# A convolution band read from a padded tap row in DRAM, early x in fp32 by a hardware queue, a smaller first weight chunk, and w_out issued early

## The chip, the cores and the metric

The kernel runs on one core of a Trainium2 chip. The metric is the device time of one execution in microseconds (us). Medians are over runs interleaved with runs of the kernel before on the same chip. A time is longer than the span of the profiled execution by 1.7 to 2.0 us; in a few runs by 2.1 to 3.5, which no profile explains. I compare kernels by times and locate the difference by spans.

## The reference

```python
# x: (8, 4096, 192) f32; weight: (8 heads, 7 taps); w_in: (192, 2048); w_out: (2048, 192)
w = softmax(weight, axis=-1)                       # per head
y[b, s, d] = sum_k w[head(d), k] * x_pad[b, s + k, d]   # causal, 6 zeros in front, 24 channels a head
h = y.reshape(32768, 192) @ w_in
g = where(h > 0, h, exp(min(h, 0)) - 1)
out = g @ w_out
```

## The kernel before

The tokens are cut into 32 blocks of 1024. A block needs 16 "pairs": for each of 16 slices of 128 hidden columns, six matmuls (three steps for each of two row tiles of 64) make two PSUM banks of h. ScalarE takes exp, GpSimd clips, VectorE joins the branches into gT (fp16), and TensorE multiplies gT by w_out. Three PSUM slots of two banks rotate among pairs and convolutions.

From block 1 on, the convolution is a matmul of x by a banded matrix, 40 small matmuls for half a block. Its result goes out of PSUM (`csb`), through DRAM (`conv_slots`) and back in another layout (`att`): the bounce. Block 0 takes another way, which needs no band and is quicker to start: x is transposed and multiplied by diagonal matrices ("the head").

What the change and the argument touch (cuts marked by `...`):

```python
# SP: the band, three transfers through DRAM
sy.dma_start(wq[...], <weight broadcast to 128 partitions>).then_inc(s_wq, 16)
W(s_tz, 1); W(s_w[0], 32)
sy.dma_start(band[:, :, :], Tm[:, :, :]).then_inc(s_band, 16)      # zeros
W(s_band, 16); W(s_set, 5)
sy.dma_start(diagonal, wprb[:]).then_inc(s_band, 16)               # taps, scattered on a diagonal
W(s_band, 32)
sy.dma_start(Tm[:], band[:, :, :]).then_inc(s_band, 16)            # the band comes back
...
# GpSimd: the software DMA queue, in this order
load_head(0); load_head(1)                   # x, cast to bf16
load_w_in(0); load_w_in(1); <xg of block 1>; load_w_in(2)
for n in range(NP):
    if n == W_OUT_AT:  <load w_out>          # W_OUT_AT = 8
    ...
# TensorE, at each item of the order
if m == 0: W(s_band, 48)                     # first convolution waits for the band
pe.matmul(H[...], xg[:, s % NXB, w, CPH*h:CPH*(h+1)], Tm[:, h, PAD+c0 : PAD+c0+nc_], ...)
...
elif n < NQ - 1: warm(WARM[1])               # block 0 only: two warming matmuls between pairs
```

## Time and profile before

| what | value |
|---|---|
| time, median of 4 runs | 760.12 us (759.85 to 763.15) |
| span of the profiled run | 758.2 us |
| TensorE busy | 742.6 us, 98% |
| first transposes / first pair / pair 16 | 8.42 / 15.42 / 43.27 us |

The prediction shows how these lines are read. The point is the last row: all of the slack lies before pair 16, the first pair of block 1, after which TensorE is full.

### The profile page before, as it was taken

The numbers are of one execution on the slowest core, as the hardware profiler recorded it, in microseconds if no ns is written. First come the engines' busy times: TensorE is split into PE (matmuls) and PEld (weight loads), VectorE is DVE, ScalarE is ACT, GpSimd is POOL, SyncE is SP. The second block draws the span as 40 slices with busy tenths as digits, with TensorE's granted clock in tenths as the row PEclk, the third lists the DMA queues.
The fourth block names the chain that finished last, engine by engine and source line by source line (L and its number), as shares of the span: only waits on it lengthen the run. The fifth ranks groups of instructions, "written<-read, shape, count | busy, mean of one in ns | idle before, by whom it ended". The sixth has DMA issues, their size and how long they took to land.

```text
span 758.2 us, 32332 instructions
## 1 busy us (share of the span) xinstructions
PE 742.6 (98%) x13911; PEld 513.4 (68%) x13911; DVE 636.8 (84%) x1043; ACT 646.9 (85%) x1161; POOL 660.6 (87%) x1107
## 2 busy tenths in 40 slices
PE   6889999999999999999999999999999999999997
PEld 4256676676767667667667667667667667667676
DVE  3778988988988988988988988988988988988993
ACT  3778888888888888888888888888888889889882
POOL 4879989989988988988988998988988998988892
PEclk9999999999999999999999999999999999999999
DMA  9643453443453453453453454354354354354112
GB/s 144 108 84 94 102 114 77 104 103 85 101 116 77 100 111 80 100 116 81 96 108 87 95 116 87 90 116 82 92 116 95 82 116 86 89 115 104 61 44 64
DMA packets 107135, 72.77 MB, mean 96 GB/s; under 512 B 44784, under 2 KB 106736, under 8 KB 106992
## 3 DMA queue, kind: packets, MB, share of 16 engines
q1 hardware_dynamic: 66344, 54.03, 23.6%
q0 software_dynamic: 40304, 16.47, 19.7%
q8 instruction: 109, 1.79, 1.0%
q14 instruction: 34, 0.28, 0.1%
q10 hardware_dynamic: 344, 0.20, 0.1%
HBM read 45.43 MB, written 41.71 MB: 115 GB/s over the span
## 4 chain that ended last, share of the span: by engine, by line
PE 95%; DMA 2%; ACT 1%; DVE 1%; POOL 1%; issue 0%; SPq 0%; POOLq 0%
PE H L628 44%; PE ops L657 44%; PE H L604 5%; DMA conv_slots<-csb 1%; DMA xh<-in_x_dram 1%; PE H L657 1%; DVE gT L499 0%; DMA att<-conv_slots 0%; PE ops L531 0%; ACT E L427 0%; PE H L579 0%; POOL E L351 0%; PE ops L579 0%; PE H L560 0%; SPq L279 0%
## 5 line engine op out<-in xcount | busy, mean ns | idle before, releaser
L499 DVE SCALAR_TENSOR_TENSOR gT<-E,H 128x512 f16<-128x512 f32 x1024 | 631.0, 682 | 98.4 <-POOL E L351 90.9
L351 POOL TENSOR_SCALAR E<-E 128x512 f32<-128x512 f32 x1024 | 604.0, 612 | 82.9 <-ACT E L427 79.3
L427 ACT ACTIVATE E<-H 128x512 f32<-128x512 f32 x1024 | 546.2, 605 | 87.4 <-PE H L628 73.8
L657 PEld LDWEIGHTS ops<-w_out,gT 64*128 64x128 f16 x8064 | 342.4, 94 | 109.6 <-ACT osb L405 10.9
L657 PE MATMUL ops<-w_out,gT 64*128 64x192 f16 x8064 | 414.4, 243 | 0.9 <-DVE gT L499 0.9
L628 PE MATMUL H<-att,w_in 64*128 64x512 bf16 x3072 | 407.3, 378 | 5.1 <-DVE gT L499 3.2
L628 PEld LDWEIGHTS H<-att,w_in 64*128 64x128 bf16 x3072 | 129.6, 94 | 107.2 <-DVE gT L499 6.0
L416 ACT ACTIVATE csb<-H 128x1024 bf16<-128x1024 f32 x62 | 63.5, 1024 | 0.0
L405 ACT ACTIVATE osb<-ops 128x768 f32<-128x768 f32 x63 | 51.6, 819 | 5.1 <-PE ops L657 5.1
L307 POOL DMA_DIRECT2D xg<-in_x_dram x62 | 52.2, 842 | 0.4 <-issue 0.4
L604 PE MATMUL H<-Tm,xg 128*24 128x122 bf16 (+1 forms) x2480 | 40.7, 209 | 0.7 <-DVE gT L499 0.7
L604 PEld LDWEIGHTS H<-Tm,xg 128*24 128x24 bf16 x2480 | 31.3, 92 | 11.3 <-issue 10.7
L531 PE MATMUL ops<-zw 128*128 128x512 bf16 x35 | 11.6, 434 | 1.2 <-DVE zw L438 1.2
L510 DVE COPY osb<-H 128x384 f32<-128x384 f32 x1 | 0.6, 558 | 8.9 <-PE H L657 8.9
L531 PEld LDWEIGHTS ops<-zw 128*128 128x128 bf16 x35 | 2.5, 106 | 7.5 <-issue 6.0
L657 PE MATMUL H<-w_out,gT 64*128 64x192 f16 x128 | 5.6, 243 | 0.1
L657 PEld LDWEIGHTS H<-w_out,gT 64*128 64x128 f16 x128 | 5.2, 94 | 0.3 <-PE H L657 0.3
L548 PE MATMUL H<-ident,xh 128*64 128x2 bf16 x12 | 0.8, 192 | 4.0 <-DMA xh<-in_x_dram 4.0
L397 ACT ACTIVATE osb<-H 128x384 f32<-128x384 f32 x1 | 0.5, 490 | 4.7 <-PE H L657 4.7
L548 PEld LDWEIGHTS H<-ident,xh 128*64 128x64 bf16 x12 | 0.7, 151 | 4.9 <-issue 4.9
L312 POOL DMA_DIRECT2D w_in<-in_moe_w_in_dram x6 | 3.8, 642 | 0.0
L463 DVE CAST xT<-H 128x512 bf16<-128x512 f32 x1 | 0.7, 692 | 3.5 <-PE H L560 3.5
(41 smaller groups left out, 26.4 us busy)
## 6 DMA issues: line engine op xcount, KB each, us to landing
out_dram<-osb SPq DMA_DIRECT2D x127, 192.0 KB, 2.7
conv_slots<-csb SPq DMA_DIRECT2D x62, 256.0 KB, 2.5
att<-conv_slots SPq DMA_DIRECT2D x186, 64.0 KB
xg<-in_x_dram POOLq DMA_DIRECT2D x31, 240.0 KB, 5.1
xg<-in_x_dram POOLq DMA_DIRECT2D x31, 192.0 KB, 4.4
w_in<-in_moe_w_in_dram POOLq DMA_DIRECT2D x4, 288.0 KB, 10.1
w_out<-in_moe_w_out_dram POOLq DMA_DIRECT2D x1, 768.0 KB, 9.9
xh<-in_x_dram POOLq DMA_DIRECT2D x2, 192.0 KB, 5.5
```

What stands on the lines that cost most here:

```text
L307: g.dma_start(xg[:, b, w0:w1, :], src).then_inc(s_x[b][part - 1], 16)
L312: g.dma_start(w_in[HP * r : HP * (r + 1), :, c0:c1], moe_w_in.rearrange("(p j) f -> p j f", j=3)[:, :, c0:c1],).then_inc(s_w[k], 16)
L351: g.tensor_scalar(out=E[:, n % NE, u, :], in0=E[:, n % NE, u, :], scalar1=1.0, scalar2=0.0, op0=ALU.min, op1=ALU.max,).then_inc(s_clp)
L405: a.activation(osb[:, b, :, :, :].rearrange("p g k d -> p g (k d)"), ops[:, :, 0 : 2 * D], ACT.Copy,).then_inc(s_oev)
L416: a.activation(csb[:, m % 4, :, :], H[:, slot_of_conv[m] % 3, :].rearrange("p (b t) -> p b t", b=2), ACT.Copy,).then_inc(s_ce)
L427: a.activation(E[:, n % NE, u, :], H[:, k, GS * u : GS * (u + 1)], ACT.Exp).then_inc(s_exp)
L499: v.scalar_tensor_tensor(out=gT[:, s % NG3, q, u, :], in0=E[:, n % NE, u, :], scalar=1.0, in1=H[:, slot_of_pair[n] % 3, GS * u : GS * (u + ...
L531: pe.matmul(ops[:, 0, :], zw[:, 0:P], zw[:], start=True, stop=True)
L548: ins = pe.matmul(halos()[HP:P, j, i, 0:HALO], xh[:, 0, i, j::3], ident[:, P - HALO : P], start=True, stop=True, tile_position=(0, HP),)
L604: ins = pe.matmul(H[SLOT * q : SLOT * q + CPH, k % 3, GS * hb + o : GS * hb + o + nc_], xg[:, s % NXB, w, CPH * h : CPH * (h + 1)], Tm[:, ...
L628: ins = pe.matmul(H[:, k % 3, GS * r : GS * (r + 1)], w_in[HP * r : HP * (r + 1), j, FC * q : FC * (q + 1)], att[HP * r : HP * (r + 1), s ...
L657: ins = pe.matmul(acc[:, g, D * kb : D * (kb + 1)], gT[HP * rt : HP * (rt + 1), t % NG3, q, g, t0 : t0 + P], w_out[HP * rt : HP * (rt + 1) ...
```

## The change

Its intent is to get TensorE to its full load sooner. In short: the band is no longer written, patched and read back, but read with a skew from a row of padded taps: partition p reads from element p on, which gives the band with its columns reversed, and the matmul reads them backwards. The early x comes as fp32 by ACT's hardware queue and is cast by ACT and VectorE. The first w_in chunk is halved. w_out is issued directly after w_in. The head uses 256 columns a matmul. More warming ahead of the head, less between the pairs, and the third convolution at n=16 instead of n=13.

```diff
-WCOLS = ((0, 512), (512, 1280), (1280, 2048))
+WCOLS = ((0, 256), (256, 1024), (1024, 2048))
-WARM = (7, 2)
+WARM = (12, 1)
-EARLY_CONV = {6: (1, 0), 9: (1, 1), 13: (2, 0)}
+EARLY_CONV = {6: (1, 0), 9: (1, 1), 16: (2, 0)}
...
-            load_head(0)
-            load_head(1)
...
+            W(s_xl[0], 16)
             load_w_in(0)
...
             load_w_in(2)
+            g.dma_start(w_out[:, :, :], ...).then_inc(s_w[3], 16)
...
+            for k in range(2):                       # ACT's queue
+                a.dma_start(xf[:, k, :, :]..., x_flat[GS * k : GS * (k + 1), :]...).then_inc(s_xl[k], 16)
...
+            W(s_xl[0], 16)
+            a.activation(xh[:, 0, :, :], xf[:, 0, :, :], ACT.Copy).then_inc(s_xha)
...
+            v.tensor_scalar(out=zt[:, CW - 1 : CW - 1 + KSIZE], in0=wde[:], scalar1=wdr[:, 0:1], ...)
+            W(s_xl[1], 16)
+            v.tensor_copy(xh[:, 1, :, :], xf[:, 1, :, :]).then_inc(s_xh)
...
-                                    Tm[:, h, PAD + c0 : PAD + c0 + nc_],
+                                    Tr[:, h, CW - c0 - nc_ : CW - c0][:, ::-1],
...
-                        warm(WARM[1])
+                        warm_pair(WARM[1])           # one pair of 64-row tiles
...
+            sy.dma_start(taps[:, :], zt[0:HP:8, :]).then_inc(s_band, 16)
+            W(s_band, 16)
+            sy.dma_start(Tr[:, :, :],
+                bass.AP(tensor=taps.tensor, offset=0, ap=[[1, P], [ZW, HEADS], [1, CW]]),
+            ).then_inc(s_band, 16)
```

More of the change, by code (lines that the diff above doesn't have):

```diff
@@ L20 @@
 SLOT = 32
-TW = 136
 CW = 122
+ZW = 256
 GS = 512
@@ L30 @@
 LAG = -1
-WCOLS = ((0, 512), (512, 1280), (1280, 2048))
-Q_PART = (0,) * 4 + (1,) * 6 + (2,) * 6
-WARM = (7, 2)
+WCOLS = ((0, 256), (256, 1024), (1024, 2048))
+Q_PART = (0,) * 2 + (1,) * 6 + (2,) * 8
+WARM = (12, 1)
 HALF_STEPS = (10, 10, 6, 6, 10, 11, 11)
 CONV_AT = ((4, 1, 1), (12, 2, 0))
-EARLY_CONV = {6: (1, 0), 9: (1, 1), 13: (2, 0)}
+EARLY_CONV = {6: (1, 0), 9: (1, 1), 16: (2, 0)}
 QUAD = 4
@@ L42 @@
 X_AT = ((5, 1), (10, 0), (13, 2))
-W_OUT_AT = 8
 PIECES = (
@@ L111, in bass_lightweight_conv__then__act_elu_kernel @@
             order.append(("h", n))
-        if s == 0:
-            convs = [EARLY_CONV[n]] if n in EARLY_CONV else []
-        else:
-            convs = [(s + ahead, g) for at, ahead, g in CONV_AT if at == i and n < NP]
+        convs = [EARLY_CONV[n]] if n in EARLY_CONV else []
+        if s:
+            convs += [(s + ahead, g) for at, ahead, g in CONV_AT if at == i and n < NP]
         convs = [(k, g) for k, g in convs if k < NS]
@@ L129, in bass_lightweight_conv__then__act_elu_kernel @@
                 conv_at(k, g)
-    band = nc.dram_tensor("conv_band", (P, HEADS, TW), BF16).ap()
+    taps = nc.dram_tensor("conv_taps", (HEADS, ZW), BF16).ap()
     bounce = nc.dram_tensor("conv_slots", (2, 2, P, SUP), BF16).ap()
@@ L156, in bass_lightweight_conv__then__act_elu_kernel @@
         xg = sbuf("xg", [P, NXB, NWIN, D], BF16)
-        Tm = sbuf("Tm", [P, HEADS, TW], BF16)
+        Tr = sbuf("Tr", [P, HEADS, CW], BF16)
         csb = sbuf("csb", [P, 4, 2, GS], BF16)
@@ L164, in bass_lightweight_conv__then__act_elu_kernel @@
         osb = sbuf("osb", [P, 2, 2, 2, D], FP32)
-        wq = sbuf("wq", [P, HEADS, KSIZE], FP32)
-        wmx = sbuf("wmx", [P, HEADS], FP32)
-        wq2 = sbuf("wq2", [P, HEADS, KSIZE], FP32)
-        wex = sbuf("wex", [P, HEADS, KSIZE], FP32)
-        wsum = sbuf("wsum", [P, HEADS], FP32)
-        wrs = sbuf("wrs", [P, HEADS], FP32)
-        wprb = sbuf("wprb", [P, HEADS, KSIZE], BF16)
+        zt = sbuf("zt", [P, ZW], BF16)
+        xf = sbuf("xf", [P, 2, QUAD, D], FP32)
         zw = sbuf("zw", [P, GS], BF16)
@@ L175, in bass_lightweight_conv__then__act_elu_kernel @@
         ops = psum("ops", [P, 2, GS])
-        s_wq = sema("s_wq")
         s_w = [sema(f"s_w{i}") for i in range(4)]
@@ L180, in bass_lightweight_conv__then__act_elu_kernel @@
         s_xl = [sema(f"s_xl{i}") for i in range(2)]
+        s_xh = sema("s_xh")
+        s_xha = sema("s_xha")
+        s_wp = sema("s_wp")
         s_id = sema("s_id")
@@ L192, in bass_lightweight_conv__then__act_elu_kernel @@
         s_hd = sema("s_hd")
-        s_set = sema("s_set")
-        s_wex = sema("s_wex")
         s_scr = sema("s_scr")
@@ L206, in bass_lightweight_conv__then__act_elu_kernel @@
         s_dw = [sema(f"s_dw{i}") for i in range(4)]
-        s_tz = sema("s_tz")
         s_band = sema("s_band")
@@ L315, in load_w_in @@
                     ).then_inc(s_w[k], 16)
-            def load_head(k):
-                g.dma_start(
-                    xh[:, k, :, :].rearrange("p i d -> p (i d)"),
-                    x_flat[GS * k : GS * (k + 1), :].rearrange("(p i) d -> p (i d)", i=QUAD),
-                ).then_inc(s_xl[k], 16)
-            load_head(0)
-            load_head(1)
             W(s_one, 1)
@@ L339, in _gpsimd @@
             load_w_in(2)
+            g.dma_start(
+                w_out[:, :, :], moe_w_out.rearrange("(q p) d -> p q d", p=FC)
+            ).then_inc(s_w[3], 16)
             for n in range(NP):
                 s, i = divmod(n, NQ)
-                if n == W_OUT_AT:
-                    g.dma_start(
-                        w_out[:, :, :], moe_w_out.rearrange("(q p) d -> p q d", p=FC)
-                    ).then_inc(s_w[3], 16)
                 for at, part in X_AT:
@@ L362, in _scalar @@
             W = Waits(a)
-            load_wd(a, 1)
+            for k in range(2):
+                a.dma_start(
+                    xf[:, k, :, :].rearrange("p i d -> p (i d)"),
+                    x_flat[GS * k : GS * (k + 1), :].rearrange("(p i) d -> p (i d)", i=QUAD),
+                ).then_inc(s_xl[k], 16)
             a.memzero(scr[:, 0:1]).then_inc(s_scr)
@@ L388, in _scalar @@
             ).then_inc(s_ha)
-            W(s_set, 2)
-            a.activation(wex[:], wq2[:], ACT.Exp).then_inc(s_wex)
             def evac(t, half):
@@ L438, in _vector @@
             v.memset(zw[:], 0.0).then_inc(s_zw)
-            v.memset(Tm[:], 0.0).then_inc(s_tz)
             v.memset(ident[:], 1.0).then_inc(s_one)
@@ L442, in _vector @@
             v.memset(Dg[:, ::8, :], 0.0).then_inc(s_z0)
+            v.memset(zt[:], 0.0).then_inc(s_z0)
             W(s_id, 1)
@@ L461, in _vector @@
             ).then_inc(s_D)
+            W(s_z0, 3)
+            v.tensor_scalar(
+                out=zt[:, CW - 1 : CW - 1 + KSIZE],
+                in0=wde[:],
+                scalar1=wdr[:, 0:1],
+                scalar2=None,
+                op0=ALU.mult,
+            ).then_inc(s_wp)
+            W(s_xl[1], 16)
+            v.tensor_copy(xh[:, 1, :, :], xf[:, 1, :, :]).then_inc(s_xh)
             W(s_tp, 3)
@@ L468, in _vector @@
             ).then_inc(s_hd)
-            W(s_wq, 16)
-            v.tensor_reduce(wmx[:], wq[:], AXIS.X, ALU.max).then_inc(s_set)
             W(s_hc, 3)
@@ L474, in _vector @@
             ).then_inc(s_hd)
-            W(s_set, 1)
-            v.tensor_tensor(
-                wq2[:],
-                wq[:],
-                wmx[:, :].unsqueeze(2).to_broadcast([P, HEADS, KSIZE]),
-                ALU.subtract,
-            ).then_inc(s_set)
-            W(s_wex, 1)
-            v.tensor_reduce(wsum[:], wex[:], AXIS.X, ALU.add).then_inc(s_set)
-            W(s_set, 3)
-            v.reciprocal(wrs[:], wsum[:]).then_inc(s_set)
-            W(s_set, 4)
-            v.tensor_tensor(
-                wprb[:, :, ::-1],
-                wex[:],
-                wrs[:, :].unsqueeze(2).to_broadcast([P, HEADS, KSIZE]),
-                ALU.mult,
-            ).then_inc(s_set)
             for n in range(NP):
@@ L531, in warm, with warm_pair @@
                     pe.matmul(ops[:, 0, :], zw[:, 0:P], zw[:], start=True, stop=True)
-            def turn(r, i, j, dst, c0):
-                return pe.matmul(
-                    dst[HP * r : HP * (r + 1)],
-                    xh[:, r % 2, i, j::3],
-                    ident[:, c0:P],
-                    start=True,
-                    stop=True,
-                )
+            def warm_pair(count):
+                for _ in range(count):
+                    for r in range(2):
+                        pe.matmul(
+                            ops[:, r, :],
+                            zw[HP * r : HP * (r + 1), 0:P],
+                            zw[HP * r : HP * (r + 1), :],
+                            start=True,
+                            stop=True,
+                            tile_position=(HP * r, 0),
+                        )
             warm(WARM[0])
             W(s_id, 1)
-            W(s_xl[0], 16)
-            W(s_xl[1], 16)
+            W(s_xha, 1)
+            W(s_xh, 1)
             for j in range(3):
@@ L575, in _tensor @@
                 for k in range(KSIZE + 1):
-                    for kb in range(2):
-                        shift, i = divmod(2 * kb - PAD + k, QUAD)
-                        for r in range(2):
-                            ins = pe.matmul(
-                                head_bank(j, r)[:, P * kb : P * (kb + 1)],
-                                Dg[HP * r : HP * (r + 1), k : k + 2, :],
-                                xT[HP * r : HP * (r + 1), j, i, HALO + shift : HALO + shift + P],
-                                start=(k == 0 and kb == 0),
-                                stop=(k == KSIZE),
-                                tile_position=(HP * r, 0),
-                                skip_group_check=True,
-                            )
+                    shift, i = divmod(k - PAD, QUAD)
+                    step = 2 * XTW if i < 2 else 1 - 2 * XTW
+                    for r in range(2):
+                        whole = xT[HP * r : HP * (r + 1), j, i, HALO + shift : HALO + shift + P]
+                        ins = pe.matmul(
+                            head_bank(j, r),
+                            Dg[HP * r : HP * (r + 1), k : k + 2, :],
+                            bass.AP(
+                                tensor=whole.tensor,
+                                offset=whole.offset,
+                                ap=[whole.ap[0], [step, 2], [1, P]],
+                            ),
+                            start=(k == 0),
+                            stop=(k == KSIZE),
+                            tile_position=(HP * r, 0),
+                        )
                 ins.then_inc(s_hc)
@@ L593, in _tensor @@
                     if m == 0:
-                        W(s_band, 48)
+                        W(s_band, 32)
                     for part in range(g + 1):
@@ L672, in _sync @@
             W = Waits(sy)
-            load_wd(sy, 0)
-            sy.dma_start(
-                wq[:, :, :].rearrange("p h k -> p (h k)"),
-                bass.AP(tensor=weight.tensor, offset=0, ap=[[0, P], [1, HEADS * KSIZE]]),
-            ).then_inc(s_wq, 16)
-            W(s_tz, 1)
-            W(s_w[0], 32)
-            sy.dma_start(band[:, :, :], Tm[:, :, :]).then_inc(s_band, 16)
-            W(s_band, 16)
-            W(s_set, 5)
-            diagonal = bass.AP(
-                tensor=band.tensor,
-                offset=0,
-                ap=[[HEADS * TW + 1, P], [TW, HEADS], [1, KSIZE]],
-            )
-            sy.dma_start(diagonal, wprb[:]).then_inc(s_band, 16)
-            W(s_band, 32)
-            sy.dma_start(Tm[:], band[:, :, :]).then_inc(s_band, 16)
+            for r in range(2):
+                load_wd(sy, r)
+            W(s_wp, 1)
+            sy.dma_start(taps[:, :], zt[0:HP:8, :]).then_inc(s_band, 16)
+            W(s_band, 16)
+            sy.dma_start(
+                Tr[:, :, :],
+                bass.AP(tensor=taps.tensor, offset=0, ap=[[1, P], [ZW, HEADS], [1, CW]]),
+            ).then_inc(s_band, 16)
             for item in order:
```

## The prediction

> **What bounds the kernel now.** I read the page first, then the chain of waits over the first 45 us, the timeline of the same stretch, a table of stretches, and the DMA issues with their landings.
>
> ```profile
> span 758.2 us, 32332 instructions
> ...
> PE 742.6 (98%) x13911; PEld 513.4 (68%) x13911; DVE 636.8 (84%) x1043; ACT 646.9 (85%) x1161; POOL 660.6 (87%) x1107
> ...
> PE 95%; DMA 2%; ACT 1%; DVE 1%; POOL 1%; issue 0%; SPq 0%; POOLq 0%
> ```
>
> From the page: TensorE has 98% of the span, and the chain that ended last is 95% TensorE. The table of stretches says where the other 2% is:
>
> ```profile
> 15.40:36.90 21.50, 19.02 (x190) 5.57 (x190) 15.81 (x28) 16.19 (x29) 16.76 (x27) 1.00 0.75 122
> 36.90:43.30 6.40, 3.72 (x78) 1.96 (x78) 4.75 (x9) 4.17 (x7) 4.97 (x9) 1.00 0.65 131
> 43.30:66.00 22.70, 22.70 (x436) 16.08 (x438) 17.93 (x30) 19.50 (x35) 18.77 (x32) 1.00 0.38 79
> 66.00:88.70 22.70, 22.70 (x436) 15.86 (x434) 19.81 (x33) 20.17 (x38) 20.61 (x36) 1.00 0.45 98
> ```
>
> Columns: stretch, length, busy time of PE, PEld, DVE, ACT, POOL. From 43.3 us on TensorE is full (22.70 of 22.70 in each block of 16 pairs). So the end is the start of pair 16, at 43.27, plus 714.9 us of TensorE work (758.2 - 43.27). The change can only (a) bring pair 16 forward, or (b) alter the 714.9. The chain up to pair 16, from the critical view:
>
> ```profile
> 1.99 6.29 DMA xh<-in_x_dram
> 8.28 0.14 issue
> 8.42 0.61 PE H L548 x9
> ...
> 10.52 1.82 PE ops L579 x32
> 12.35 2.52 PE H L579 x64
> ...
> 15.42 0.82 PE H L628 x6
> ...
> 30.65 1.04 ACT csb L416
> 31.69 0.02 issue
> 31.71 6.84 DMA conv_slots<-csb
> ...
> 39.82 3.41 DMA att<-conv_slots
> 43.23 0.05 issue
> 43.27 0.82 PE H L628 x6
> ```
>
> Columns: start, duration, what. So: x arrives at 8.28; 7.0 us of transposes and a convolution by diagonals (the "head") until the first pair at 15.42; 24.9 us to pair 15 at 40.33; and a bounce of the second block's convolution through DRAM, which lands at 43.23.
>
> **What the Trainium skill says.**
> 1. "TensorE: Matmul & The Clock Gate", section "What's actually happening": the array starts at half clock and is released after some 3.4 us of sustained activity, falling back when idle for as long. The trace agrees: the 7 warming matmuls take 434 ns (mean) and end near 4.4; the transposes at 8.4 are cold again; the first 32 head matmuls take 1.82 us, 114 ns per pair of row tiles, where 128 columns at full clock would be 53. Counts per half microsecond rise from about 15 to 26 only near 13.7: some 5.3 us after 8.42.
> 2. "DMA: Bandwidth & Descriptors", section "SWDGE vs HWDGE vs iDMA": only the software path casts. That is why the early x on a hardware queue comes as fp32 and needs two copies. The trace has x on the software queue: issued at 1.29 and 1.99, landed after 4.8 and 6.3.
> 3. "VectorE: DVE Perf Modes", section "Mode 2×_2P — use both read ports for one tensor": an fp32 SBUF copy makes two elements a cycle. My estimate for its 768 columns is therefore 0.45 to 0.8 us; no instruction of this trace shows it.
> 4. "SBUF — State Buffer", section "Door 1: The DMA port swizzle (why `[64,N]` ≈ `[32,N]`)": reads are fast as long as at least two fall into the same 16-byte line. A step of minus one stays eight bf16 in a line, so I expect reversed columns to be free. No run shows this yet.
>
> **The change, part by part.**
>
> *x arrives.* The two issues on ACT's queue start near 0.8; ACT's first issue now takes 1.21 us. A 256 KB store lands 2.5 us after issue in the steady part; for 384 KB of fp32 I take 4.5 and 5.8. ACT copies its half after the small Exp (now at 5.42; the taps come by two issues on SP, so perhaps 0.3 later): 768 columns as in the osb eviction, 0.82 us, so about 6.9. VectorE's half comes last: taps 5.1, Dg until 6.9 (0.69 us), zt 0.3, copy 0.45 to 0.8: about 7.9 against 8.42. Gain 0.5 only, because the weight chain and not x now sets the moment.
>
> *Head.* Twelve warming matmuls at 0.43 last until about 6.4 instead of 4.4; if they release the clock, it is full at 7.9. Head convolution: 48 matmuls of 256 columns instead of 96 of 128, the same columns, 24 pairs of row tiles. Warm: 0.75 us to the first transposed third, 0.65 to copy it (0.60 on ACT), 24 x 107 ns = 2.6, last copy and handover 0.55: 4.6 us. Cold: much as today, 7.0, less what is released on the way. I give warm 0.6 and take 5.3 us as mean: first pair at 13.2 instead of 15.42, gain 2.2. w_in's first chunk, issued only after x has landed (4.7) but half the size, should land near 9.5, in time (today 9.3 and 10.7).
>
> *Pairs 0 to 15.* Today's distance is 1.293 us; TensorE's two warming matmuls and their mode change are 0.54 of it (chain: 16.24, 0.54). The paired one takes about 0.21, so the distance falls to what VectorE allows: 12 instructions in 7.26 us at 54.63, 0.605 each, 1.21 per pair. I take 1.22: 15 x 0.07 = 1.05 gained. Each convolution in this stretch costs about 1.8 (pair 6 to pair 7: 23.17 to 26.24, less 1.29); moving the third to n=16 gains 1.8 here and adds 0.59 (40 matmuls, 49.67 to 50.26) to the full part. By compute alone pair 16 would start at 13.2 + 15 x 1.22 + 2 x 1.8 + 1.65 (pair 15 and its 20 output matmuls, 40.33 to 41.98) = 36.8.
>
> *Bounce.* Today the store of m=1 takes 6.84 instead of 2.5 because w_out was issued at 28.91 and takes 9.9:
>
> ```profile
> conv_slots<-csb SPq DMA_DIRECT2D x62, 256.0 KB, 2.5
> ...
> w_out<-in_moe_w_out_dram POOLq DMA_DIRECT2D x1, 768.0 KB, 9.9
> ```
>
> Now w_out follows w_in. The software queue moved 2352 KB of results (xh 384, w_in 1536, xg 432; w_in is loaded twice) from about 4.0 to 19.5: 152 KB/us. From 6.5 it needs (1536 + 432)/152 = 13 us, until 19.5, then w_out 8 us (30.8 to 38.8 today): until 27.5. So w_out leaves the store of m=1 but meets that of m=0 (near 23), which may then land near 29; its three reads block SP until 31; m=1's store follows, 2.6, until 33.6; three issues 1.3; 3.4 to land: about 38.2. Half the overlap gone gives 36.6. I take 37.6 for pair 16.
>
> *Band.* Removed: a 272 KB write, a scattered 14 KB write and a 272 KB read (issued 10.83, 17.58, 21.13; 6.7, 3.5, 2.7 us), eight small VectorE and ACT instructions of 0.2. Added: a 4 KB row write and a read of 1024 pieces of 244 B. It was needed at 24.2 and came with 0.7 us of visible wait on the weight side, behind other waits: worth nearly nothing. It should now be there by 15.
>
> Sum: 43.27 - 37.6 = 5.7 gained, 0.6 given back: 5.1. 760.25 - 5.1 = 755.2 us.
>
> **Rivals.**
> - *Reversed columns stream at half rate.* 62 convolutions of 0.59 us, four column tiles at once: 0.45 more each, 28 us, 788. For: no access of this trace is reversed. Against: point 4. Chance 0.07.
> - *The bounce replaces the head.* w_out against m=0 holds pair 16 near 39.5: gain 3.2, about 757. For: today's 6.84 store. Against: w_out would be done by then if the early queue is faster.
> - *Nothing waits.* Warm head, w_out out of the way: first pair 12.5, pair 16 at 36: gain 6.7, about 753.5.
> - *The lighter warming lets the clock fall.* Pairs at half clock would take 1.7 instead of 1.22, 7 us over 15: about 762. Against: TensorE still works 0.86 of 1.22 us. Chance 0.05.
> - *w_in comes late*, since it waits for x: pair 2 needs the second chunk, by my rate near 12.5 to 13.5, against 15.6. Two microseconds of slack; being late would cost 1 to 2 us.
>
> **Range and chances.** The gain lies between 3 and 7.5 us in all but the rivals of chance 0.07 and 0.05, and even the whole 43 us up to pair 16 cannot shrink by 15 us (2%), for 22 us of pair work remain in it. So: 755.2, range 751.8 to 758.0; faster 0.02, same 0.91, slower 0.07.
>
> **What would show it.** Right: the first transposes near 7.9 and released by the VectorE copy; head pairs at 107 ns; first pair 12.5 to 13.5; pairs 1.22 apart; m=0's store slow, m=1's 2.5; pair 16 near 37.6; TensorE full afterwards with 40 convolution matmuls still in 0.59. Wrong if the convolution's mean of 209 ns or its 0.59 grows, if pair 16 starts after 41, or if TensorE shows idle time after pair 16.

## The result, and the profile after

The changed kernel takes 755.94 us (median of 4, 754.96 to 756.65) against 760.12: ratio 0.9935, 95% interval 0.9906 to 0.9964. Ratios are the mean time of one kernel's runs over that of the other's of the same rounds, so not quite the ratio of the medians. The result is correct. The forecast was 755.2.

The page of the changed kernel, its span and the shares of the chain that ended last:

```profile
span 753.2 us, 32238 instructions
...
PE 94%; DMA 3%; DVE 1%; POOL 1%; ACT 0%; issue 0%; SPq 0%
```

The span is 5.0 us shorter, and TensorE is still 94% of the chain, but DMA has a larger share of it than before, which one would not expect of a change that removes transfers. The table of stretches of the changed kernel (stretch, length, busy time of PE, PEld, DVE, ACT and POOL with instruction counts, TensorE's granted clock, DMA share, GB/s):

```profile
6.00:8.00 2.00, 0.10 (x3) 0.13 (x3) 1.45 (x4) 0.97 (x3) 2.00 (x3) 1.00 1.09 135
8.00:10.00 2.00, 2.00 (x40) 1.76 (x41) 0.66 (x1) 1.02 (x3) 2.00 (x4) 0.67 1.07 123
10.00:12.00 2.00, 2.00 (x24) 1.39 (x20) 0.03 (x1) 0.78 (x2) 1.38 (x2) 0.50 1.04 114
...
14.00:35.00 21.00, 16.00 (x198) 6.20 (x198) 15.79 (x27) 16.82 (x32) 16.72 (x28) 1.00 0.90 146
35.00:40.00 5.00, 4.31 (x96) 2.91 (x98) 4.35 (x8) 3.96 (x7) 4.83 (x9) 1.00 0.48 73
40.00:62.70 22.70, 22.70 (x436) 15.85 (x432) 18.70 (x31) 20.39 (x37) 19.48 (x34) 1.00 0.50 110
```

Two things are to be seen. From 40 us TensorE is full again, 22.70 of 22.70, as before. And the clock column falls to 0.50 while the head runs. The chain of waits up to pair 16, changed kernel (start, duration, what):

```profile
7.16 0.15 DVE zt L451
7.31 0.02 issue
7.33 5.45 DMA conv_taps<-zt
12.78 0.02 issue
12.79 10.98 DMA Tr<-conv_taps
23.77 0.04 issue
23.82 0.65 PE H L589 x35
...
37.34 0.82 PE H L613 x6
```

Before, this chain ran through x, the head, the pairs and the bounce. In this profile the head is not in it at all: it runs through the tap row and the band, 16.4 us of DMA, to the first convolution, and from there through the pairs (cut here), with GpSimd and VectorE between them. The same moment in the timeline:

```profile
23.82 0.65 PE L589 MATMUL H<-Tr,xg 128*24 128x122 bf16 x40 [1.67 <-DMA Tr<-conv_taps]
```

TensorE stood 1.67 us in front of the first convolution because the band was not there. Yet that wait cost next to nothing. In e1 (below), the same kernel once more, TensorE waits 1.37 us for the band, but the chain does not touch the band; it runs through the head, GpSimd's clips and its issue of an x load to pair 7:

```profile
15.91 3.50 POOL E L335 x6
...
21.82 0.87 POOL xg L299
...
24.72 0.84 PE H L613 x6
```

And in e11, where the band is in time, pair 7 waits for VectorE instead:

```profile
24.61 0.82 PE L612 MATMUL H<-att,w_in 64*128 64x512 bf16 x6 [0.99 <-DVE gT L476]
```

Pair 7 starts at 24.62 here, at 24.72 in e1 and at 24.61 in e11. Two paths end together there, and a chain shows only the one that ended last. The first store, which follows the first convolution, does go out earlier in e11 (24.41 instead of 25.59), but pair 16 does not start earlier for it.

Pair 16 starts at 37.34 instead of 43.27, 5.9 us earlier. From there to the end it is 715.9 us (753.2 - 37.34) against 714.9: 1.0 is given back, 0.59 of it the 40 matmuls of the third convolution, which now come after pair 16. 5.9 less 1.0 is the whole difference of the spans, rounding aside.

Reversed columns cost nothing. The convolution's group before, and after:

```profile
L604 PE MATMUL H<-Tm,xg 128*24 128x122 bf16 (+1 forms) x2480 | 40.7, 209 | 0.7 <-DVE gT L499 0.7
```

```profile
L589 PE MATMUL H<-Tr,xg 128*24 128x122 bf16 (+1 forms) x2480 | 40.6, 209 | 2.4 <-DMA Tr<-conv_taps 1.7
```

The mean of one is 209 ns both times; what is new is the idle time ahead and its releaser.

### The profile page after: what moved, and what is told of

It reads as the page before. It is cut to its first block, busy times and chain, and to the rows that moved or that the text cites. A ratio compares the mean times of both kernels' runs of the same rounds, so it can differ in the third digit from the quotient of the medians.

```text
span 753.2 us, 32238 instructions
## 1 busy us (share of the span) xinstructions
PE 739.3 (98%) x13868; PEld 512.3 (68%) x13868; DVE 635.2 (84%) x1040; ACT 647.3 (86%) x1161; POOL 661.4 (88%) x1105
## 4 chain that ended last, share of the span: by engine, by line
PE 94%; DMA 3%; DVE 1%; POOL 1%; ACT 0%; issue 0%; SPq 0%
PE ops L642 45%; PE H L613 44%; PE H L589 5%; DMA Tr<-conv_taps 1%; DVE gT L477 1%; PE H L642 1%; DMA conv_taps<-zt 1%; POOL E L335 1%; DMA wd<-in_weight_dram 1%; ACT E L415 0%; SPq L234 0%; POOL xg L299 0%; DVE Dg L442 0%; ACT osb L393 0%; DVE osb L488 0%
## 5 line engine op out<-in xcount | busy, mean ns | idle before, releaser
L404 ACT ACTIVATE csb<-H 128x1024 bf16<-128x1024 f32 x62 | 63.5, 1024 | 1.4 <-PE H L589 1.3
L589 PE MATMUL H<-Tr,xg 128*24 128x122 bf16 (+1 forms) x2480 | 40.6, 209 | 2.4 <-DMA Tr<-conv_taps 1.7
L589 PEld LDWEIGHTS H<-Tr,xg 128*24 128x24 bf16 x2480 | 31.1, 92 | 12.8 <-issue 10.6
L509 PE MATMUL ops<-zw 128*128 128x512 bf16 x12 | 4.7, 577 | 1.2 <-DVE zw L426 1.2
L514 PE MATMUL ops<-zw 64*128 64x512 bf16 x28 | 5.4, 377 | 0.0
```

What stands on the lines that cost most here:

```text
L404: a.activation(csb[:, m % 4, :, :], H[:, slot_of_conv[m] % 3, :].rearrange("p (b t) -> p b t", b=2), ACT.Copy,).then_inc(s_ce)
L509: pe.matmul(ops[:, 0, :], zw[:, 0:P], zw[:], start=True, stop=True)
L514: pe.matmul(ops[:, r, :], zw[HP * r : HP * (r + 1), 0:P], zw[HP * r : HP * (r + 1), :], start=True, stop=True, tile_position=(HP * r, 0),)
L589: ins = pe.matmul(H[SLOT * q : SLOT * q + CPH, k % 3, GS * hb + o : GS * hb + o + nc_], xg[:, s % NXB, w, CPH * h : CPH * (h + 1)], Tr[:, ...
```

## The experiments

Twelve kernels ran, each in five rounds (e4 and e6 have six runs) with the kernel before beside it. All gave the right result. The table has their times, and of each profiled run three moments and the rest of the span after pair 16.

| run | time, median (range) | before | ratio (95%) | first pair | wait for band | pair 16 | rest |
|---|---|---|---|---|---|---|---|
| e1_again: the change | 755.29 (754.72 to 756.26) | 760.26 | 0.9937 (0.9924 to 0.9950) | 14.35 | 1.37 | 37.47 | 715.6 |
| e2_wout_at8 | 759.05 (758.31 to 760.33) | 760.26 | 0.9986 (0.9972 to 0.9999) | 14.20 | 0.89 | 40.90 | 715.7 |
| e3_warm_old | 755.50 (755.26 to 757.13) | 760.26 | 0.9940 (0.9926 to 0.9954) | 14.72 | 0.72 | 39.67 | 715.7 |
| e4_clock | 755.93 (754.95 to 757.93) | 760.26 | 0.9947 (0.9932 to 0.9962) | 13.04 | 3.14 | 38.84 | 715.7 |
| e5_gate | 756.88 (756.41 to 758.15) | 759.99 | 0.9966 (0.9954 to 0.9978) | 14.57 | none | 39.41 | 717.0 |
| e6_clock_conv8 | 756.83 (755.67 to 759.12) | 759.99 | 0.9963 (0.9951 to 0.9975) | 13.55 | none | 38.67 | 715.7 |
| e7_band_only | 757.86 (757.45 to 758.96) | 759.99 | 0.9980 (0.9967 to 0.9993) | 13.55 | none | 41.02 | 714.7 |
| e8_wout_only | 762.67 (762.36 to 763.07) | 759.99 | 1.0039 (1.0027 to 1.0051) | 15.19 | 4.16 | 46.05 | 714.9 |
| e9_x_sw | 754.84 (753.62 to 756.51) | 760.29 | 0.9930 (0.9916 to 0.9944) | 11.62 | about 3.5 | 37.88 | 715.6 |
| e10_band_wout | 756.10 (755.13 to 756.68) | 760.29 | 0.9946 (0.9933 to 0.9958) | 14.83 | none | 40.11 | 714.8 |
| e11_direct | 755.26 (754.67 to 755.90) | 760.29 | 0.9936 (0.9922 to 0.9950) | 14.24 | none | 37.72 | 715.7 |
| e12_direct_clock | 756.06 (755.28 to 756.74) | 760.29 | 0.9947 (0.9935 to 0.9960) | 13.44 | 1.34 | 38.60 | 715.7 |

The last column is the strongest reading. Whatever was done to the first 40 us, the rest is 714.7 to 714.9 us where the third convolution is at n=13 (e7, e8, e10) and 715.6 to 715.7 where it is at n=16. Only e5 is off, since its clock was taken back just after pair 16. (In the first profile of the changed kernel it is 715.9.) So in these runs the start of pair 16 is all that a change to the opening moved. The profiled run is one of several, so its moments and the median need not agree to better than a microsecond (e3's profiled run was its slowest).

### e1_again: the changed kernel once more

> The changed kernel itself, as the base for the others of this call. Both theories: 755 to 757 us, first pair near 14.2 us, 40 convolution matmuls of the first block waiting for the band until about 23.8, pair 16 near 37.3. If the head's clock is a matter of where a 3.41 us window falls, the half-clock stretch will lie elsewhere or be longer or shorter than the 8.66 to 12.07 of the first profile, and the times will spread by 1 to 2 us with it.

No edit. 755.29 us, band waited for until 23.67, pair 16 at 37.47. The half-clock stretch lay elsewhere, from about 9.3 to 12.7. The effect is confirmed.

### e2_wout_at8: w_out back at pair 8

```diff
-            g.dma_start(w_out[:, :, :], ...).then_inc(s_w[3], 16)
             for n in range(NP):
+                if n == 8:
+                    g.dma_start(w_out[:, :, :], ...).then_inc(s_w[3], 16)
```

> w_out issued at pair 8 again, everything else changed. Theory A (the early w_out has two effects: it frees the store of m=1, and it slows the band's read, which then holds the first convolution): the band lands before 21 us instead of 23.8, the first convolution waits for nothing (1.7 us regained), but the store of m=1 takes 6 to 7 us instead of 2.5 and pair 16 starts at 39 to 40: 757.5 to 758.5 us. Rival B (w_out's place is of no account, since the store is hidden behind the pairs): pair 16 within 0.5 of 37.3 and 755.5 to 756.5.

759.05 us, 3.8 more than e1 in the same rounds: without the early w_out most of the gain is gone. The store of block 1's second half took 7.0 us instead of 2.6, and in the timeline of this run pair 16 waits for the bounce:

```profile
40.90 0.82 PE L614 MATMUL H<-att,w_in 64*128 64x512 bf16 x6 [2.67 <-DMA att<-conv_slots]
```

Half of theory A fell: the band came only 0.6 us sooner, at 23.0. So in the changed kernel it is not w_out that makes the band late, but the rest of the software queue.

### e3_warm_old: the old warming between pairs

```diff
-                        warm_pair(WARM[1])
+                        warm(2)
```

> Two full-array warming matmuls between the pairs of the first block again instead of one pair of row tiles. Theory A (TensorE with its mode change set the distance of 1.29 us; but the first six pairs hide behind the late band): distance 1.29 instead of 1.20, the convolution at n=6 still at 23.8, and only the nine pairs after it pay, 0.8 us: 756.5 to 757. Rival B (VectorE sets the distance): distance 1.20 and no change.

The distance between pairs is 1.29 us again instead of 1.20, so TensorE's warming did set it; whether by its length or by the change from row tiles to the full array and back was not separated. The time is 755.50 against 755.29, no difference clear of the noise. In this profile the band is waited for 0.72 us and the bounce 1.56 us.

### e4_clock: the clock held up to the head

```diff
             warm(WARM[0])
+            W(s_v, 3)
+            warm(4)
+            W(s_D, 1)
+            warm(2)
```

> Six more warming matmuls, gated by events of the weight chain, fill the gap of 1.9 us before x, so that the clock isn't taken back in the head. Theory A (the late band holds everything): the head shortens, first pair at 12.5 to 13 instead of 14.2, but the first convolution still waits for the band until about 23.8 (wait 3 us instead of 1.7) and pair 16 moves by less than 0.4: 755.5 to 756.5, with less spread. Rival B (the head sets pair 16): 1.4 us faster, 754 to 755. Should the clock be cold anyway through another window, the fillers cost up to 0.7 us of head.

The head became as short as hoped: clock 1.00 throughout, first pair at 13.04 instead of 14.35. Nothing of it arrives. In this run's timeline the first convolution waits as long as it must, and then runs at half speed (1.04 us instead of 0.65), the granted clock having fallen to 0.50 at the end of the wait (23.77 to 27.19):

```profile
24.14 1.04 PE L593 MATMUL H<-Tr,xg 128*24 128x122 bf16 x40 [3.14 <-DMA Tr<-conv_taps]
```

755.93 us, no better than e1. Theory A holds. Here, unlike in the changed kernel, the band does bind: pair 7 starts at 25.51. In this profile pair 16 starts even later than in e1, at 38.84, so the wait and the half clock took back more than the head had saved; over all runs the times do not differ clearly.

### e5_gate: the last w_in chunk and w_out only after the tap row

```diff
                 load_x(1, part)
+            W(s_band, 16)
             load_w_in(2)
```

> The changed kernel, but GpSimd issues the last chunk of w_in and w_out only once the tap row has landed (near 12.6 us), in time it has free. Theory A (the band's read waits behind the packets of the software queue): the tap row lands a little earlier, the read's first packets move near 14 instead of 16.6, the band lands by 18 to 20 us, the first convolution waits for nothing, and pair 16 comes 1 to 1.5 us earlier, unless the later w_out (landing near 30) now slows the stores: 754 to 755.5 us. Rival (the read's 1024 small pieces are slow by themselves): the band still lands after 22.5 and nothing moves.

The wait for the band is gone (the convolution starts at 22.98, held by VectorE). The band landed at 17.8, 4.8 us after its issue instead of 11.0 in e1, so theory A is right about the band and its rival falls. But w_out now runs beside the store of the first half, which takes 5.3 us instead of 2.9; SP, which issues in order, gets to the second store only at 31.96 instead of 30.28; and pair 16 starts at 39.41, just after the bounce has landed (39.37). 756.88 us, slower than e1: the bounce now binds.

### e6_clock_conv8: the clock held, the convolutions two pairs later

```diff
-EARLY_CONV = {6: (1, 0), 9: (1, 1), 16: (2, 0)}
+EARLY_CONV = {8: (1, 0), 10: (1, 1), 16: (2, 0)}
```

(with the edit of e4)

> The fillers that keep the clock, with the first two convolutions moved from pairs 6 and 9 to pairs 8 and 10, so that TensorE has pairs to do while the band is under way. Theory A (the head's gain was swallowed by the wait for the band): first pair near 13, wait for the band under 1 us, pair 16 near 36.5 or earlier: 753.5 to 754.7 us. Rival (pair 16 hangs on the bounce whatever comes before): the later convolutions make the bounce later, pair 16 at 38 or more, 756 or more.

The rival was right. No wait for the band and pair 15 already at 34.62, but pair 16 at 38.67 after 2.41 us of waiting for the bounce; 756.83 us. Once the band no longer binds, the later bounce does.

### e7_band_only: the kernel before with the new band alone

The edit is the part of the change that concerns `band`, `Tm`, `wq` and their chain of small instructions; all else is the kernel before.

> The kernel before with the new band alone (tap row, skewed read, reversed columns; all else as before). Theory A (reversed columns cost nothing and the band is not what the kernel before waits for): 759.5 to 760.7 us, same convolution time of 0.59 us for 40 matmuls; the band's read, behind the software queue until about 19.5, lands near 22, before the 24.2 at which it is used. Rival 1 (reversed reading is slower): 28 us more. Rival 2 (the band is where the change gains): 757 to 758.

757.86 against 759.99: 2.1 us faster (1.5 by the ratio, whose interval means 0.5 to 2.5), where my theory said nothing would happen. The convolution is not slower, so rival 1 falls for good. Rival 2 has the size, but not by way of the band's own wait. Here is how TensorE got x, timeline of this run:

```profile
7.35 0.57 PE L536 MATMUL H<-ident,xh 128*64 128x2 bf16 x9 [2.99 <-DMA xh<-in_x_dram]
```

x is there at 7.35 instead of 8.42, by the same software queue. Of what the new band removes, only one transfer is issued before 7 us: the broadcast of the weights to 128 partitions (`wq`, 128 small packets, 5.7 us from issue to landing). These packets move between 5 and 7.3 us. From 5 to 7 us the software queue moves 178 packets beside them, and 326 in e7, though x was issued at the same moments in both (1.29 and 1.99). Runs with it have the first transposes at 8.42 (before) and 8.55 (e8); without it and with x on the same queue, at 7.35 (e7), 7.45 (e10) and 6.52 (e9). So the broadcast is the likely cause; it was not taken out alone. The first pair was at 13.55, partly because this run's clock was released early (0.51 at 10 to 11, 1.00 from 11 on).

### e8_wout_only: the kernel before with the early w_out alone

```diff
             load_w_in(2)
+            g.dma_start(w_out[:, :, :], ...).then_inc(s_w[3], 16)
             for n in range(NP):
-                if n == W_OUT_AT: ...
```

> The kernel before with w_out issued right after w_in, all else as before. Theory A (the early w_out is the largest part of the gain, but it slows the band's path): the store of m=1 takes 2.5 to 3 instead of 6.8, the 1.3 us wait before pair 16 goes and 1.2 us of issue time leaves GpSimd's loop, but the old band's last two transfers (17.6 to 23.8 in the profile of before) now run beside w_out and come 1 to 3 us later, which takes part of it back: 757.5 to 759.5 us. Rival (without the shorter head the early w_out gains nothing): 760.

762.67 us, 2.7 slower. The old band's last two transfers took 6.06 and 3.37 us instead of 3.5 and 2.7, and the band came at 27.9. So here the early w_out does slow the band. Timeline of this run:

```profile
27.92 1.04 PE L603 MATMUL H<-Tm,xg 128*24 128x122 bf16 x40 [4.16 <-DMA Tm<-conv_band]
```

TensorE waits 4.16 us, loses its clock (1.04 us again, and the next pairs 1.46), and pair 16 starts at 46.05.

### e9_x_sw: x by the software queue again

The edit puts the two loads of the kernel before back on GpSimd and drops the two fp32 loads and their copies.

> The changed kernel with x loaded by the software queue and cast on the way, as before, instead of fp32 by ACT's queue with two copies. Theory A (in the run with the band alone x landed near 7.2 by the software queue, since the transfers for the old band no longer ran beside it; so the hardware path gains little): first transposes at 7.3 to 7.6 instead of 7.7 to 7.9, pair 16 still held by the band, 755 to 756.3 us. Rival (the hardware path is a part of the gain): first transposes at 8.3 or later and 0.5 to 1 us slower, 756 to 757.

754.84 us, ratio 0.9930 against 0.9937 of e1: the hardware path of x is no part of the gain. x even came sooner: first transposes at 6.52, first pair at 11.62, 2.7 us ahead of e1. All of that is lost in one wait of some 3.5 us for the band, which came at 23.1, and in the half clock after it (23.6 to 27.0).

### e10_band_wout: new band and early w_out, nothing else

The edits of e7 and e8 together.

> The kernel before with the new band and the early w_out together, nothing else. Alone the band gave 2.1 us and the early w_out cost 2.7. Theory A (the two belong together: the short path of the band makes the early w_out bearable): no 4 us wait for the band, store of m=1 near 2.5, no wait for the bounce before pair 16; but the third convolution still at n=13 and pairs 1.29 apart, so pair 16 at 40 to 41.2: 756.5 to 757.9 us. Rival (parts add up): 760.0 - 2.1 + 2.7 = 760.6 us.

756.10 us against 760.29: 4.2 us, somewhat better than theory A said; added up, the parts would have given a loss of 0.6. The two belong together. With the short band the early w_out harms nothing, and pair 16 waits for no bounce (40.11, right behind the pairs). Whether the other edits together add anything is not shown: e1 gained 5.0, the first measurement of the same kernel 4.2, and the intervals of e1 and e10 overlap.

### e11_direct: the skewed rows straight from SBUF

```diff
-            sy.dma_start(taps[:, :], zt[0:HP:8, :]).then_inc(s_band, 16)
-            W(s_band, 16)
-            sy.dma_start(Tr[:, :, :], <skewed read of taps>).then_inc(s_band, 16)
+            for h in range(HEADS):
+                row = zt[8 * h : 8 * h + 1, 0:CW]
+                sy.dma_start(Tr[:, h, :],
+                    bass.AP(tensor=row.tensor, offset=row.offset, ap=[row.ap[0], [1, P], [1, CW]]),
+                ).then_inc(s_band, 16)
```

> The changed kernel with the skewed rows read straight from the padded tap rows in SBUF, by eight transfers, instead of by a tap row in DRAM (one hop of 5.5 us less). Theory A (the band's second hop behind the software queue holds the first convolution): the eight are issued at 7.1 to 10.5, land by 18 to 21, the first convolution no longer waits, pair 16 1 to 1.5 us earlier, 36 to 36.5: 754 to 755 us. Rival (pair 16 is bound by the pairs and the bounce alike): the wait goes, pair 16 stays at 37 to 37.5 and the time at 755 to 756.

The rival was right. The band no longer holds the convolution (22.65, behind VectorE), and pair 16 starts at 37.72 after 0.73 us of waiting for the bounce; 755.26 us, as e1. In the changed kernel VectorE releases pair 16 (the PSUM slot is free at 37.19, at 37.32 in e1), and the bounce has landed only shortly before (36.96; 36.67 in e1). The band, as shown above, ends together with the pairs at pair 7.

### e12_direct_clock: the same with the clock held

The edits of e11 and e4.

> The same with the fillers that keep the clock in the head. Theory A: first pair near 13, no wait for the band, so now the shorter head reaches pair 16, at 34.8 to 35.8: 753 to 754.3 us, the fastest of all. Rival: the last store and its three reads land no earlier than 37, wait before pair 16 of 1.5 us or more, 755 us.

756.06 us. First pair at 13.44, but pair 16 at 38.60. The chain of waits of this run and its timeline name the reason:

```profile
34.50 4.06 DMA att<-conv_slots
```

```profile
38.60 0.82 PE L616 MATMUL H<-att,w_in 64*128 64x512 bf16 x6 [2.41 <-DMA att<-conv_slots]
```

The last read of the bounce takes 4.06 us, though the pairs before it were done earlier. GpSimd's load of the next x is issued at 33.65, just ahead of it; that this load delays the read is likely and was not tested. Of the versions tried none is clearly faster than the changed kernel.

## Why the prediction was right

The time (755.2 forecast, 755.94 and 755.29 measured) was right, and so was the frame: the end is the start of pair 16 plus a constant. Predicted pair 16: 37.6; measured 37.34 and 37.47. But two of its steps were wrong, the band (nearly 9 us late, at no cost in the end) and the head (1.0 us), and that the total held is in part luck: two other terms came out better than said.

**The band failed.** "It should now be there by 15" was wrong: it landed at 23.8. I had counted bytes (a 4 KB row, a 244 KB read) and not packets in a loaded queue. The packet records of e1's trace show it: the tap row is issued at 7.12, its first packets move at 10.9, the read is issued at 12.62 and its first packet moves at 16.3, its last of 1024 at 23.2. One of its packets takes about 31 ns, so 64 on each of 16 engines are 2 us of work. But between 17 and 21 us each microsecond holds about as many packets of the software queue as of the band (115 and 116, 164 and 163, 201 and 203, 269 and 247), as if each band packet waited for one software packet. These take about 75 ns on average, so my estimate is 64 times (31 + 75), 6.8 us, and the measured stretch is 6.9. e5 tests this: with the rest of the software queue held back, the first packet of the read moves 1.1 us after its issue (13.00 to 14.07) and all 1024 in 3.4 us. The Trainium skill states that an engine takes turns between queues by whole packets ("DMA: Bandwidth & Descriptors", section "Queues, rings and completion order"). A packet there holds several descriptors, a record of the trace is one piece of 244 or 384 bytes; the equal counts agree with equal turns, but how long a turn is they do not show.

"Worth nearly nothing" holds in so far as even the late band cost nothing (pair 7 at 24.62 with the wait and 24.61 without), but not of what the band's removal does elsewhere: e7 shows 2.1 us, with x landing 1.1 us sooner, and e8 and e10 show that only the new band lets w_out go first.

**x by the hardware queue.** The moment was right (7.9 forecast, 7.91, released by VectorE's copy, which took 0.55 us where 0.45 to 0.8 was estimated). The worth was not in it: e9 is as fast without it.

**The head was mis-sized.** 5.3 us forecast as a mean of two cases, 6.3 measured (7.91 to 14.20). The twelve warming matmuls did release the clock, but it was taken back at 8.68 and returned at 12.10, 3.41 us later. In the window before, 5.27 to 8.68, TensorE was busy for 1.49 us only, for the warming ended at 5.98 and x came at 7.91. e4 shows the cure and its worth: first pair at 13.04, and nothing gained, because then the band binds.

**Pair distance, bounce and early w_out held.** 1.20 us for 1.22 forecast, and e3 puts it back to 1.29. The store of the second half took 2.5 us as said; the first half's took 3.0 and not the 6 I feared, and the first three pairs came 0.86 us apart, since the three PSUM slots are empty at first. The first three pairs won back 0.7 of the head's 1.0: pair 15 started at 35.32, where the sum has 35.1. The 0.8 put on top for the bounce was not paid by it, since it landed at 36.96, before VectorE released pair 16; the last step, pair 15 to 16, took 2.02 instead of 1.65. So errors of up to 1 us cancelled. Of the rivals, "the bounce replaces the head" comes closest in e5 (pair 16 at 39.41, with w_out beside the first store) and holds in part in e2, e6 and e12, though not in the changed kernel.

**Where the gain comes from**, then, in steps that were each measured against the kernel before: new band alone 2.1 us (1.5 by the ratio); with the early w_out 4.2; with all the rest 4.2 and 5.0 in two measurements, so that the rest adds anything is not shown. The early w_out alone loses 2.7, and taking it out of the changed kernel costs 3.8.

**What stays open.** Why the last bounce read takes 4 us in e12; whether the early x, the head, the warming and the place of the third convolution gain anything together; whether a band read in fewer and longer pieces would pass the software queue faster; and the executions with one microsecond or more outside the span.

## What to carry to other kernels

Price a small transfer beside a busy queue by its packets, each with one packet of the competitor, plus the time until its first one moves (3.7 us here, 1.1 where the queue was held back), and not by its bytes. A wait for a late transfer is not yet a cost: look for what the engine would have waited for next. When several chains end within a microsecond of each other, shortening one of them gives only the distance to the next: test parts alone and together, since here one part loses alone and makes a large part of the gain in company. And a matmul engine that waits long enough may then run at half clock, as after the waits of 3.1 and 4.2 us in e4 and e8, which can use up a saving upstream.

## What the Trainium skill lacked or had wrong

- "DMA: Bandwidth & Descriptors", section "Latency and other measured facts", gives about 600 ns to the first byte of a hardware-queue transfer. Beside a loaded software queue it was about 3.7 us in e1, twice in a row (issued 7.12, first packets at 10.9; issued 12.62, first packet at 16.3). The page has no figure for this case.
- "TensorE: Matmul & The Clock Gate", section "What's actually happening", has the clock fall after an idle window of some 3.4 us. Here it fell after a window in which TensorE was busy for 1.49 of 3.41 us (44%), in e1 after one with 1.80 (53%). The page does not say how little counts as idle. The length of the window agrees: 3.41 us of half clock, 8.68 to 12.10.
- No page says that the clock column of a profile reads 1.00 until the first recorded transition. Before the change it shows 1.00 at 8.4 to 13.7 us, while TensorE started 14 matmuls in half a microsecond (13.0 to 13.5), and 26 after the transition (14.0 to 14.5).
- No page says what a moving operand read backwards costs. Nothing: 209 ns mean with and without, over 2480 matmuls.
